# Six weight stores of a top-k attention and two-MLP kernel, moved from the preparation to the first product and behind a load of k

## The chip, the cores and the metric

The kernel runs on one core of a Trainium2 chip, as one launch. The metric is the device time of an execution in microseconds (us), and the median of several executions is compared. A core has five engines with instruction streams of their own: PE (matmul; its weight loads are shown as PEld), DVE (vector), ACT (scalar), POOL (GpSimd) and SP, which here issues every DMA. Each engine runs its stream strictly in the order in which it was written, and waits where an operand is not there yet.

## The reference

Attention in which each query keeps only its 32 largest scores, then two feed-forward layers without residuals.

```python
scores = scale * np.matmul(q, k.transpose(0, 1, 3, 2))     # 4 batches, 8 heads, 576 x 576, head size 64
kth = np.partition(scores, -top_k, axis=-1)[..., -top_k:-top_k + 1]
scores = np.where(scores >= kth, scores, -1000000000.0)
attn = softmax(scores)
x = np.matmul(attn, v)                                     # laid out as 2304 tokens x 512
h = x @ w_in;  x = (h - np.tanh(h)) @ w_out                # 512 -> 2048 -> 512
h = x @ w_in2; out = np.where(h > 0, h, np.exp(np.minimum(h, 0)) - 1) @ w_out2
```

The inputs of the attention are float32. The weights of the two layers are float64.

## The kernel before, in words

**Tiling.** The 2304 tokens are cut into 6 chunks of 384. For each chunk the attention is done pair of heads by pair of heads (4 pairs, two groups of three 128-row score tiles each), and then both layers run over 16 f-tiles of 128 columns each. The layers of a chunk run while the attention of the next chunk is under way. `m` is the layer (0 or 1), `ft` the f-tile, `ci` the chunk.

**Top-k.** For every score tile DVE takes four times the 8 largest values (`topk_steps`, L406) and three times removes them (L420); the threshold then masks the exponentials (`e`, L427 on DVE, L422/L423 on ACT). PE transposes `e` (L448), ACT copies it (`ph`, L449), PE multiplies with v (`av`, L470), and the normalized result is split into a high and a low part `xh`, `xl` (L148, L149).

**Weights.** PE works on words that are split into a high and a low part, which takes three products instead of one. `prepare(m, ft)` (L177 to L213) makes them once: SP loads the 1 MB of raw words `wr` (L180), ACT scales them (L186) and converts the low halves (L203), DVE joins both into `wf` (L189), ACT and POOL split that into `wp` (`split`, L147 to L149), and SP stores `wp`, 1 MB, to the DRAM scratch `w` (L213). Chunk 0 uses `wp` where it lies; chunks 1 to 5 load the words back as `wt` (`load_next`, L215, L222). `wp` and `wt` share one ring of `W2_BUFS` = 6 buffers (`weight_tile`, L172). So the seventh tile can only be written when the first is free: its product in `second` (L613) is done and every DMA that reads it has landed.

**Which tiles when.** Nine tiles (`EARLY`, numbers 12 to 20 of 32) are prepared in the first ticks and only stored. The first six of layer 0 (`AHEAD` = 6, `ft` 0 to 5) are prepared in the last ticks before the layers of chunk 0 begin, and stay in the ring. The rest follow while the layers of chunk 0 run: each step `c` of `step_parts` (L651) calls `first` of the next f-tile (L566; products `h`, L577, then `t`, L580), `gate` (L586), `second` (L602) and `load_next`.

**Loads of k.** `load_k` (L303) loads raw k as `kraw`; from chunk 1 on it comes in two halves (L316), in a ring of two buffers that is freed by the split into `kk`. `kraw1_1_1_0_0_1` is chunk 1, pair 1, batch 1, from query 0, head 1 of the pair; a number behind it in an order is the tile's running number. `sd`, `qraw`, `vraw` are the stores of parked scores and the loads of q and v.

**What sets the order.** The program writes the work in ticks (L731 to L773), and a scheduler then orders each engine's stream by its own estimate of when operands are ready. `tc.issue_after(x)`, used through `behind(kind)` (L153), keeps what is written under it behind `x` on its queue. A changed DMA thus also changes the order that the scheduler writes on the other engines. Once written, the order is fixed.

Of the kernel before, what the change touches and what calls it, by code (L numbers as in the profile page):

```python
# [19 lines left out]
B, H, S, D = 4, 8, 576, 64  # L20
# [7 lines left out]
NF = DFF // P  # L28
# [19 lines left out]

EARLY = range(12, 21)
PREP_AT = 8
PREP_RATE = 2.5
AHEAD = 6
# [52 lines left out]
def tile_topk_attention_two_mlps(  # L107
# [9 lines left out]
    nc = tc.nc  # L117
# [10 lines left out]
    def mlp_tile(shape, dt, **kw):  # L128
        if "open" in pools:
            opening.close()  # L130
            del pools["open"]
            pools["mlp"] = pool("mlp", 1)
        return pools["mlp"].tile(shape, dt, **kw)
# [10 lines left out]
    def f(ap):  # L144
        return ap.bitcast(F32)

    def split(hi, lo, src):  # L147
        nc.scalar.activation(hi, src, copy)  # L148
        return nc.gpsimd.tensor_sub(lo, src, f(hi))  # L149

    newest = {}

    def behind(kind):  # L153

        return tc.issue_after(newest[kind].ins) if kind in newest else nullcontext()

    def bank(tag, name, bufs):
        if tag == "h":
            if "park" in pairs:
                turns.close()  # L160
                del pairs["park"]
                pairs["h"] = pool("ph", 1, PSUM)
            return pairs["h"].tile([P, 512], F32, tag=tag, name=name, bufs=bufs)
        return ps.tile([P, 512], F32, tag=tag, name=name, bufs=bufs)


    scratch = {
        (m, ft): dr.tile([P, 2, 2, 512], F32R, tag=f"w{m}_{ft}", name=f"w{m}_{ft}") for m in range(2) for ft in range(NF)
    }
    weights, loads = {}, [(ci, m, ft) for ci in range(len(SIZES)) for m in range(2) for ft in range(NF)]  # L170

    def weight_tile(name):  # L172
        return sb.tile([P, 2, 2, 512], F32R, tag="w", name=name, bufs=W2_BUFS)
# [3 lines left out]
    def prepare(m, ft):  # L177

        raw = sb.tile([P, 1024], I64, tag="wr", name=f"wr{m}_{ft}", bufs=RAW_BUFS)
        nc.sync.dma_start(raw, (w1, w2)[m][ft])  # L180
        words = raw.bitcast(F32).rearrange("p (n w) -> p n w", w=2)
        low, scaled = words.bitcast(U32)[:, :, 0], words[:, :, 1]
        w = sb.tile([P, 1024], F32, tag="wf", name=f"wf{m}_{ft}", bufs=WF_BUFS)

        def scale(out, src):
            nc.scalar.activation(out, src, AF.Prelu, scale=2.0**-112, alpha=-(2.0**32))  # L186

        def join(out, high, low):
            nc.vector.scalar_tensor_tensor(  # L189
                out.bitcast(U32), high.bitcast(U32), 3, low, op0=ALU.logical_shift_left, op1=ALU.bitwise_or  # L190
            )

        halves = [slice(0, 512), slice(512, 1024)]
        small = {}
        early = "wide" in stage
        if early:
            for a, cs in enumerate(halves):
                small[a] = bank(f"acc{stage['at'] % 3}", f"sc{m}_{ft}_{a}", 1)
                stage["at"] += 1
                scale(small[a], scaled[:, cs])  # L200
        else:
            scale(scaled, scaled)
        nc.scalar.activation(low.bitcast(I32), low, copy, scale=2.0**-29 * (1 - 2.0**-20), bias=-0.5 + 7.5 * 2.0**-20)  # L203
        if early:
            for a, cs in enumerate(halves):
                join(w[:, cs], small[a], low[:, cs])
        else:
            join(w, scaled, low)
        wt = weight_tile(f"wp{m}_{ft}")
        if m * NF + ft not in EARLY:  # L210
            weights[0, m, ft] = wt
        split(wt[:, :, 0], wt[:, :, 1], w.rearrange("p (h c) -> p h c", h=2))
        nc.sync.dma_start(f(scratch[m, ft]), f(wt))  # L213

    def load_next():  # L215
        if loads:
            ci, m, ft = loads.pop(0)
            if ci == 0 and m * NF + ft not in EARLY:
                prepare(m, ft)
                return  # L220
            wt = weights[ci, m, ft] = weight_tile(f"wt{ci}_{m}_{ft}")
            newest["weights"] = nc.sync.dma_start(f(wt), f(scratch[m, ft]))  # L222
# [10 lines left out]
    for ci, size in enumerate(SIZES):  # L233
        for p in range(NPAIR):
            row = []
            c0 = 0
            for b, q0, n in CHUNKS[ci]:
                for heads in ([[0], [1]] if n >= 256 else [[0, 1]]):
                    u = Unit()
# [10 lines left out]
            cuts, k = [], 0  # L250
# [28 lines left out]
    def parked(u):  # L279

        return u.g.at in PARK
# [3 lines left out]
    def wide(u):  # L285

        return u.whole or parked(u)
# [15 lines left out]
    def load_k(u):  # L303
        if wide(u):
            if u.heads[0] == 0:
                tag, bufs = ("kp", 1) if parked(u) else ("kraw", KR_BUFS)
                k = pair_k[u.ci, u.p] = (pools["open"] if parked(u) else sb).tile([P, S], F32, tag=tag, name=f"kw{u.id}", bufs=bufs)
                for h in range(2):
                    nc.sync.dma_start(k[h * D : h * D + D], kT[u.b, 2 * u.p + h])
            u.kraw = pair_k[u.ci, u.p]  # L310
            return
        u.kraw = {}
        for h in u.heads:
            u.kraw[h] = sb.tile([P, S], F32, tag="kraw", name=f"kraw{u.id}_{h}", bufs=KR_BUFS)
            for half in range(2):
                nc.sync.dma_start(u.kraw[h][half * D : half * D + D], kT[u.b, 2 * u.p + h])  # L316

    def split_qk(u):

# [246 lines left out]
    def first(ci, m, ft):  # L566
        n = SIZES[ci]
        xh, xl = x_tiles[ci] if m == 0 else z_tiles[ci]
        h = bank("h", f"h{ci}_{m}_{ft}", 2)[:, :n]
        wv = weights[ci, m, ft][:, 0].rearrange("p a (k c) -> p a k c", c=P)  # L570
        jobs = [(wi, xs, kt) for wi, xs in ((0, xh), (1, xh), (0, xl)) for kt in range(4)]
        if m == 0 and ft == 0:
            jobs.sort(key=lambda x: x[2])
        late = (n // P - 1) * P
        for cs in (slice(0, late), slice(late, n)) if m == 1 and ft < PARTED and late else (slice(0, n),):
            for a, (wi, xs, kt) in enumerate(jobs):
                nc.tensor.matmul(h[:, cs], wv[:, wi, kt], xs[:, kt, cs], start=(a == 0), stop=(a == len(jobs) - 1))  # L577
        t = mlp_tile([P, NMAX], F32, tag="t", name=f"t{ci}_{m}_{ft}", bufs=T_BUFS)[:, :n]
        if m == 0:
            nc.scalar.activation(t, h, AF.Tanh)  # L580
        else:
            nc.scalar.activation(t, h, AF.Relu, scale=-1.0)  # L582
            nc.scalar.activation(t, t, AF.Exp, scale=-1.0)  # L583
        parts[ci, m, ft] = h, t
# [106 lines left out]
    for g in groups:  # L691
        t0 = 4 * g.at
        for u in g.units:
            lead = 6 if u.whole else 8
            if parked(u):
                at = PARK_AT + PARK_STEP * parks[0]
                parks[0] += 1
                on(before, int(at) - 3, lambda u=u: (load_q(u), load_k(u)))
                for t in range(u.k):
                    on(ends, int(at + t * PARK_STEP / 3), lambda u=u, t=t: later(park, u, t))  # L700
            else:
                on(before, max(-6, t0 - lead) if u.whole else t0 - lead, lambda u=u: (load_q(u), load_k(u)))
                on(before, t0 - 5, lambda u=u: split_qk(u))
            on(before, t0 + (1 if hurried(u) else 3), lambda u=u: load_v(u))
        for blk in range(NB):
            if not hurried(g.units[-1]):
                on(late, t0 + 4 + (1 if g.units[0].ci == 1 else 0) + (0 if quick(g.units[-1]) else blk // 3), lambda g=g, blk=blk: transposed(g, blk))
        for j, (u, t) in enumerate(g.tiles):
            on(mid, t0 - 4 + j, lambda u=u, t=t: scores(u, t))
        for u in g.units:  # L710
            if hurried(u):
                continue
            if u.last:
                on(ends, t0 + (5 if quick(u) else 7), lambda u=u: norm(u.ci, u.p, u))
                on(ends, t0 + (5 if quick(u) else 7), lambda u=u: attend(u))
                if spread(u):
                    on(ends, t0 + 8, lambda u=u: load_rs(u))
                    on(ends, t0 + 10, lambda u=u: finish_pair(u))
                else:
                    on(ends, t0 + (5 if quick(u) else 7), lambda u=u: finish_pair(u))  # L720
# [8 lines left out]

    early = list(EARLY)  # L730
    for tick in range(FIRST_TICK, n_ticks):  # L731
        for do in before.get(tick, ()):
            do()
        while early and PREP_AT + PREP_RATE * (len(EARLY) - len(early)) <= tick:
            i = early.pop(0)
            prepare(i // NF, i % NF)
        if starts[0] - AHEAD <= tick < starts[0]:
            load_next()
        if tick == starts[0]:
            first(*steps[0])  # L740
            gate(*steps[0])
# [71 lines left out]
```

## Time and profile before

| | |
|---|---|
| median of 3 runs | 1216.76 us (1215.71 to 1218.65) |
| profiled execution, its own time | 1219.57 us |
| its span, first to last instruction | 1217.8 us |
| PE busy | 1146.4 us (94%) |
| DVE busy | 944.5 us (78%) |
| ACT busy | 765.6 us (63%) |
| POOL busy | 497.9 us (41%) |
| bytes moved by DMA | 301.69 MB, mean 248 GB/s |

The profile shows one execution. Busy is the time in which an engine ran instructions; an idle engine waits for what the brackets in a timeline row name. Shares of the whole span mix stages with different limits, so stretches are read apart: the opening to about 160 us (attention of chunk 0 alone, weights prepared), the stretch to about 205 us in which the layers of chunk 0 start, and what follows. "Issue to landing" of a DMA is from its issue by SP until all of its bytes are there. "Granted clock" is TensorE's clock as the throttle granted it, as a share of full speed.

### The profile page before, as it was taken

To read this page: it belongs to the slowest core of one execution; us is meant where nothing else is said; L and a number is where in the kernel's file an instruction comes from. 1 tells how busy PE (TensorE), PEld (TensorE's weight loads), DVE (VectorE), ACT (ScalarE), POOL (GpSimd) and SP (SyncE) were. 2 spreads that over 40 slices of the span, in tenths; PEclk is the share of its full clock that TensorE was granted. 3 is DMA by queue.
4 is the path that set the end of the run, shared out by engine and by line. 5 is a ranking of instruction groups with operands and counts; after the bars stand their busy time and mean duration, and the time that the engine had idled before them with its cause. 6 is when DMAs were issued, how large, how long until landed. Compare 5 with 4: busy or idle time off the path is not lost.

```text
span 1217.8 us, 18856 instructions
## 1 busy us (share of the span) xinstructions
PE 1146.4 (94%) x6349; PEld 977.0 (80%) x6349; DVE 944.5 (78%) x1898; ACT 765.6 (63%) x1594; POOL 497.9 (41%) x557
## 2 busy tenths in 40 slices
PE   6577689999999999999999999999999999999998
PEld 3344368888888979898978988988998888898887
DVE  7999999998999999679987789898889995100111
ACT  5999987888984555565664566575655564432333
POOL 2445446657753313443423444444334422333222
PEclk9688889999999999999999999999999999999999
DMA  7999937985979986669986779978688645686572
GB/s 246 398 333 330 311 111 276 350 266 217 356 285 327 276 294 184 238 166 299 241 182 234 242 204 260 251 219 266 225 241 243 204 127 207 210 283 248 198 269 95
DMA packets 81616, 301.69 MB, mean 248 GB/s; under 512 B 18800, under 2 KB 36080, under 8 KB 51696
## 3 DMA queue, kind: packets, MB, share of 16 engines
q1 hardware_dynamic: 81520, 300.49, 76.5%
q8 instruction: 50, 0.82, 0.3%
q14 instruction: 46, 0.38, 0.1%
HBM read 255.07 MB, written 45.39 MB: 247 GB/s over the span
## 4 chain that ended last, share of the span: by engine, by line
PE 75%; ACT 6%; DVE 5%; DMA 3%; issue 1%; POOL 1%; another core or an unknown queue 0%; ACTq 0%; DVEq 0%; POOLq 0%
PE h L577 30%; PE acc L613 30%; PE av L470 6%; PE pt L448 5%; DMA wt<-w 3%; PE ps L383 2%; PE ps L384 2%; DVE vm L406 2%; DVE w L420 2%; DVE wf L189 1%; ACT ph L449 1%; ACT s L385 1%; ACT e L410 1%; ACT y L627 1%; ACT wr L186 0%
## 5 line engine op out<-in xcount | busy, mean ns | idle before, releaser
L149 POOL TENSOR_TENSOR gl<-g,gh 128x384 fp32r<-128x384 f32 x192 | 205.3, 1071 | 385.0 <-ACT gh L148 360.2
L406 DVE MAX8 vm<-w 128x8 f32<-128x576 f32 x432 | 315.0, 748 | 3.1
L613 PE MATMUL acc<-wt,gh 128*128 128x512 f32 x1014 | 270.9, 398 | 0.3 <-ACT gh L148 0.3
L613 PEld LDWEIGHTS acc<-wt,gh 128*128 128x128 f32 x1014 | 186.2, 188 | 34.9 <-issue 3.3
L420 DVE MATCH_REPLACE8 w<-vm,w 128x576 f32<-128x576 f32 x288 | 212.7, 740 | 0.0
L148 ACT ACTIVATE gh<-g 128x384 fp32r<-128x384 f32 x192 | 100.7, 525 | 81.2 <-DVE g L591 34.6
L613 PE MATMUL acc<-wt,gl 128*128 128x512 f32 x507 | 148.9, 398 | 1.0 <-POOL gl L149 1.0
L577 PE MATMUL h<-zh,wt 128*128 128x384 f32 (+2 forms) x776 | 146.4, 324 | 2.4 <-ACT zh L632 2.0
L591 DVE SCALAR_TENSOR_TENSOR g<-t,h 128x384 f32<-128x384 f32 x96 | 52.2, 544 | 124.2 <-ACT t L583 123.8
L406 DVE MAX8 vm<-s 128x8 f32<-128x576 f32 x144 | 107.2, 750 | 47.1 <-ACT s L385 44.4
L577 PE MATMUL h<-xh,wt 128*128 128x384 f32 x672 | 140.9, 339 | 1.2 <-DMA wt<-w 1.2
L385 ACT ACTIVATE s<-ps 128x288 f32<-128x288 f32 (+1 forms) x272 | 107.5, 418 | 48.3 <-PE ps L384 40.7
L449 ACT ACTIVATE ph<-pt 116x384 f32<-116x384 f32 (+1 forms) x240 | 111.5, 499 | 40.0 <-PE pt L448 37.4
L448 PE MATMUL pt<-ident,e 128*116 128x128 f32 (+1 forms) x720 | 115.2, 288 | 22.7 <-ACT e L423 9.9
L577 PEld LDWEIGHTS h<-zh,wt 128*128 128x128 f32 x776 | 125.8, 189 | 8.8 <-ACT zh L632 3.2
L448 PEld LDWEIGHTS pt<-ident,e 128*116 128x116 f32 (+1 forms) x720 | 90.0, 142 | 43.2 <-ACT e L423 12.6
L577 PEld LDWEIGHTS h<-xh,wt 128*128 128x128 f32 x672 | 117.4, 188 | 7.5 <-ACT t L580 1.0
L582 ACT ACTIVATE t<-h 128x384 f32<-128x384 f32 x96 | 46.8, 489 | 119.7 <-PE h L577 119.7
L613 PEld LDWEIGHTS acc<-wt,gl 128*128 128x128 f32 x507 | 93.3, 188 | 19.9 <-POOL gl L149 1.2
L420 DVE MATCH_REPLACE8 w<-vm,s 128x576 f32<-128x576 f32 x144 | 106.7, 741 | 0.0
L596 DVE TENSOR_TENSOR g<-h,t 128x384 f32<-128x384 f32 x76 | 41.4, 545 | 70.6 <-ACT t L580 69.9
L580 ACT ACTIVATE t<-h 128x384 f32<-128x384 f32 x96 | 47.2, 492 | 75.1 <-PE h L577 74.6
(82 smaller groups left out, 1938.7 us busy)
## 6 DMA issues: line engine op xcount, KB each, us to landing
wt<-w SPq DMA_DIRECT2D x169, 1024.0 KB, 6.5
wr<-in_w_dram SPq DMA_DIRECT2D x32, 1024.0 KB, 7.2
w<-wp SPq DMA_DIRECT2D x32, 1024.0 KB, 8.5
kraw<-in_kT_dram SPq DMA_DIRECT2D x96, 144.0 KB, 6.2
vraw<-in_vL_dram SPq DMA_DIRECT2D x64, 160.0 KB, 4.5
sd<-sp SPq DMA_DIRECT2D x24, 288.0 KB, 7.3
s<-sd SPq DMA_DIRECT2D x24, 288.0 KB, 9.0
qraw<-in_qT_dram SPq DMA_DIRECT2D x64, 96.0 KB, 5.7
```

The source lines that it names most:

```text
L148: nc.scalar.activation(hi, src, copy)
L149: return nc.gpsimd.tensor_sub(lo, src, f(hi))
L385: nc.scalar.activation(s[lo:hi, cs], pt[lo:hi, :HS], copy)
L406: nc.vector.max(g.vm[:, j, min(r, 1)], u.s[t] if r == 0 else g.w[j])
L420: nc.vector.match_replace(g.w[j], v, u.s[t] if r == 0 else g.w[j], FILL)
L448: nc.tensor.transpose(pt[:kn, j * P : j * P + P], v.e[t][:, k0 : k0 + kn], ident)
L449: nc.scalar.activation(g.ph[:kn, blk, :nq], pt[:kn, :nq], copy)
L470: nc.tensor.matmul(banks[c0][h * D : h * D + D, : v.n], v.vraw[h][:kn, blk], v.g.ph[:kn, blk, cs], start=(blk == order[0]), stop=(blk == o ...
L577: nc.tensor.matmul(h[:, cs], wv[:, wi, kt], xs[:, kt, cs], start=(a == 0), stop=(a == len(jobs) - 1))
L580: nc.scalar.activation(t, h, AF.Tanh)
L591: nc.vector.scalar_tensor_tensor(g, t, -1.0, h, op0=ALU.add, op1=ALU.max)
L613: nc.tensor.matmul(acc[ci, m][t], gx[:, t * P : t * P + P], wt[:, wi], start=(ft == 0 and k == 0), stop=(ft == NF - 1 and k == 2),)
```

## The change

For the tiles with a number under `AHEAD` (layer 0, `ft` 0 to 5) `prepare` no longer issues the store but keeps the tile in `kept`. `first(ci, m, ft)` issues it when the tile's first product is written, under `behind("k")`, so behind the half of a `kraw` tile that was written last by then. The other 26 stores stay in `prepare`. No instruction is added or taken away.

```diff
--- before.py
+++ after.py
@@ -48,7 +48,7 @@
 
 
 
-EARLY = range(12, 21)
+EARLY = range(12,21)
 PREP_AT = 8
 PREP_RATE = 2.5
 AHEAD = 6
@@ -210,7 +210,12 @@
         if m * NF + ft not in EARLY:
             weights[0, m, ft] = wt
         split(wt[:, :, 0], wt[:, :, 1], w.rearrange("p (h c) -> p h c", h=2))
-        nc.sync.dma_start(f(scratch[m, ft]), f(wt))
+        if m * NF + ft < AHEAD:
+            kept[m, ft] = wt
+        else:
+            nc.sync.dma_start(f(scratch[m, ft]), f(wt))
+
+    kept = {}
 
     def load_next():
         if loads:
@@ -313,7 +318,7 @@
         for h in u.heads:
             u.kraw[h] = sb.tile([P, S], F32, tag="kraw", name=f"kraw{u.id}_{h}", bufs=KR_BUFS)
             for half in range(2):
-                nc.sync.dma_start(u.kraw[h][half * D : half * D + D], kT[u.b, 2 * u.p + h])
+                newest["k"] = nc.sync.dma_start(u.kraw[h][half * D : half * D + D], kT[u.b, 2 * u.p + h])
 
     def split_qk(u):
 
@@ -568,6 +573,9 @@
         xh, xl = x_tiles[ci] if m == 0 else z_tiles[ci]
         h = bank("h", f"h{ci}_{m}_{ft}", 2)[:, :n]
         wv = weights[ci, m, ft][:, 0].rearrange("p a (k c) -> p a k c", c=P)
+        if (m, ft) in kept:
+            with behind("k"):
+                nc.sync.dma_start(f(scratch[m, ft]), f(kept.pop((m, ft))))
         jobs = [(wi, xs, kt) for wi, xs in ((0, xh), (1, xh), (0, xl)) for kt in range(4)]
         if m == 0 and ft == 0:
             jobs.sort(key=lambda x: x[2])
```

The first place is SP's queue. Before, the stores of tiles 0 to 5 (`w0_0` to `w0_5`) stand one by one among the loads of the opening; the last three of them:

```order
L213 DMA w0_3_80<-wp0_3_1469 128x2048
L295 DMA qw2_3_1_192_1_1048<-in_qT_dram 64x384
L301 DMA qraw1_0_0_384_0_1003<-in_qT_dram 64x2x192 x2
L180 DMA wr0_6_1650<-in_w1_dram 128x1024
L213 DMA w0_4_81<-wp0_4_1506 128x2048
L356 DMA sd2_3_1_192_0_2_1177<-sp2_3_1_192_0_2_1172 128x576
L316 DMA kraw1_0_1_0_0_0_1182<-in_kT_dram 64x576 x2
L180 DMA wr0_7_1733<-in_w1_dram 128x1024
L301 DMA qraw1_0_1_0_0_1179<-in_qT_dram 64x2x192 x2
L213 DMA w0_5_82<-wp0_5_1544 128x2048
L356 DMA sd2_3_1_192_1_0_1245<-sp2_3_1_192_1_0_1240 128x576
L180 DMA wr0_8_1798<-in_w1_dram 128x1024
```

Now the six stand far behind `wr0_9`, and the queue runs so around them:

```order
L321 DMA kraw1_1_1_0_0_1_1561<-in_kT_dram 64x576 x2
L578 DMA w0_0_77<-wp0_0_1305 128x2048
L578 DMA w0_1_78<-wp0_1_1349 128x2048
L578 DMA w0_2_79<-wp0_2_1377 128x2048
L578 DMA w0_3_80<-wp0_3_1466 128x2048
L578 DMA w0_4_81<-wp0_4_1502 128x2048
L321 DMA kraw1_2_0_384_0_0_1876<-in_kT_dram 64x576 x2
L306 DMA qraw1_2_1_0_0_2188<-in_qT_dram 64x2x192 x2
L321 DMA kraw1_2_0_384_0_1_1879<-in_kT_dram 64x576 x2
L578 DMA w0_5_82<-wp0_5_1539 128x2048
```

Five stores follow one another behind the second half of `kraw1_1_1_0_0_1`, ahead of the next k; the sixth stands two k tiles further on. The loads `wr0_3` to `wr0_9` moved up: `wr0_8` and `wr0_9` now stand ahead of `kraw1_0_1_0_0_1`.

The second place is DVE at the end of chunk 0's last group (names with `0_3`), into which the first group of chunk 1 (`1_0`) is woven. Before:

```order
L406 MAX vm0_3_0_3_0_0_1_1202<-w30_3_0_3_0_0_1_2_1207 128x8
L406 MAX vm1_0_1_0_0_384_0_1441<-s1_0_0_384_0_0_1213 128x8
L420 MATCH_REPLACE w30_3_0_3_0_0_1_2_1207<-vm0_3_0_3_0_0_1_1202,w30_3_0_3_0_0_1_2_1207 128x576
L420 MATCH_REPLACE w31_0_1_0_0_384_0_0_1444<-vm1_0_1_0_0_384_0_1441,s1_0_0_384_0_0_1213 128x576
L406 MAX vm0_3_0_3_0_0_1_1202<-w30_3_0_3_0_0_1_2_1207 128x8
L406 MAX vm1_0_1_0_0_384_0_1441<-w31_0_1_0_0_384_0_0_1444 128x8
L427 SCALAR_TENSOR_TENSOR e0_3_0_0_1_2_1251,sum0_3_0_3_0_0_1_1204<-s0_3_0_0_1_2_1102,vm0_3_0_3_0_0_1_1202,e0_3_0_0_1_2_1251 128x576
L420 MATCH_REPLACE w31_0_1_0_0_384_0_0_1444<-vm1_0_1_0_0_384_0_1441,w31_0_1_0_0_384_0_0_1444 128x576
L501 RECIPROCAL r0_3_1413<-r0_3_1413 128x6
```

And now:

```order
L411 MAX vm1_0_1_0_0_384_0_1438<-w31_0_1_0_0_384_0_0_1441 128x8
L411 MAX vm1_0_1_0_0_384_0_1438<-s1_0_0_384_0_1_1259 128x8
L411 MAX vm0_3_0_3_0_0_1_1202<-w30_3_0_3_0_0_1_2_1207 128x8
L425 MATCH_REPLACE w31_0_1_0_0_384_0_0_1441<-vm1_0_1_0_0_384_0_1438,w31_0_1_0_0_384_0_0_1441 128x576
L411 MAX vm1_0_1_0_0_384_0_1438<-s1_0_0_384_0_2_1312 128x8
L425 MATCH_REPLACE w31_0_1_0_0_384_0_1_1442<-vm1_0_1_0_0_384_0_1438,s1_0_0_384_0_1_1259 128x576
L432 SCALAR_TENSOR_TENSOR e0_3_0_0_1_2_1251,sum0_3_0_3_0_0_1_1204<-s0_3_0_0_1_2_1102,vm0_3_0_3_0_0_1_1202,e0_3_0_0_1_2_1251 128x576
L411 MAX vm1_0_1_0_0_384_0_1438<-w31_0_1_0_0_384_0_0_1441 128x8
L425 MATCH_REPLACE w31_0_1_0_0_384_0_2_1443<-vm1_0_1_0_0_384_0_1438,s1_0_0_384_0_2_1312 128x576
L411 MAX vm1_0_1_0_0_384_0_1438<-w31_0_1_0_0_384_0_1_1442 128x8
L506 RECIPROCAL r0_3_1410<-r0_3_1410 128x6
```

The last mask `e0_3_0_0_1_2` went from place 206 to 210 of DVE's stream, the reciprocal `r0_3` from 208 to 214, and `xl0` (the end of chunk 0's attention) from 227 to 230, since more rows of `1_0` stand ahead of them.

The third place is ACT where the ninth and tenth tile are split (`wp0_8`, `wp0_9`) and the layers of chunk 0 are at f-tile 4 and 5. Before:

```order
L148 ACTIVATE kk1_2_0_384_0_0_2092<-kraw1_2_0_384_0_0_1877 128x576
L449 ACTIVATE ph1_0_1_0_0_384_0_1708<-pt1_0_1_0_0_384_0_3_1779 116x384
L148 ACTIVATE wp0_8_1804<-wf0_8_1800 128x2x512
L580 ACTIVATE t0_0_4_1836<-h0_0_4_1823 128x384
L148 ACTIVATE wp0_9_1870<-wf0_9_1866 128x2x512
L449 ACTIVATE ph1_0_1_0_0_384_0_1708<-pt1_0_1_0_0_384_0_4_1784 112x384
L186 ACTIVATE wr0_10_1935<-wr0_10_1935 128x1024
L203 ACTIVATE wr0_10_1935<-wr0_10_1935 128x1024
L580 ACTIVATE t0_0_5_1902<-h0_0_5_1889 128x384
```

And now:

```order
L148 ACTIVATE wp0_8_1802<-wf0_8_1798 128x2x512
L588 ACTIVATE t0_0_4_1835<-h0_0_4_1821 128x384
L454 ACTIVATE ph1_0_1_0_0_384_0_1705<-pt1_0_1_0_0_384_0_3_1777 116x384
L454 ACTIVATE ph1_0_1_0_0_384_0_1705<-pt1_0_1_0_0_384_0_4_1782 112x384
L148 ACTIVATE kk1_2_0_384_0_0_2092<-kraw1_2_0_384_0_0_1876 128x576
L427 ACTIVATE e1_0_1_0_0_0_1656<-s1_0_1_0_0_0_1449,nk1_0_1_0_1_0_0_1819 128x576
L427 ACTIVATE e1_0_1_0_0_1_1657<-s1_0_1_0_0_1_1477,nk1_0_1_0_1_0_0_1819 128x576
L415 ACTIVATE e1_1_0_384_0_2_1947<-s1_1_0_384_0_2_1760,mb1_1_1_1_0_384_0_1883 128x576
L148 ACTIVATE wp0_9_1869<-wf0_9_1865 128x2x512
L428 ACTIVATE e1_0_1_0_0_0_1656,sum1_0_1_0_1_0_0_1592<-e1_0_1_0_0_0_1656,b21_0_1_0_1_0_0_1820 128x576
L588 ACTIVATE t0_0_5_1902<-h0_0_5_1888 128x384
```

Between `wp0_9` and `t0_0_5` one `e` stands instead of one `ph` and both conversions of `wr0_10`, which went 17 places further down; `kk1_2_0_384_0_0` moved behind `wp0_8`, and three `e` moved ahead of `wp0_9`.

On every engine the order differs from the opening to the third chunk's layers, and is the same from there to the end.

## Rows read from the trace of the kernel before

**Rows 1.** The page: DMA share in 40 slices of 30.4 us, stores (KB each, us to landing).

```profile
DMA  7999937985979986669986779978688645686572
...
w<-wp SPq DMA_DIRECT2D x32, 1024.0 KB, 8.5
```

**Rows 2.** Windows: stretch, length, busy of PE, PEld, DVE, ACT, POOL, clock, DMA, GB/s.

```profile
80.00:150.00 70.00, 48.00 (x187) 29.09 (x186) 67.04 (x128) 67.66 (x132) 33.09 (x41) 0.84 0.94 335
150.00:190.00 40.00, 35.64 (x185) 29.43 (x186) 38.04 (x78) 32.36 (x67) 20.57 (x22) 0.89 0.39 123
210.00:640.00 430.00, 424.33 (x2516) 367.24 (x2517) 393.81 (x798) 289.86 (x601) 194.84 (x223) 1.00 0.83 263
640.00:1217.80 577.80, 569.01 (x3210) 503.92 (x3206) 355.30 (x724) 296.39 (x646) 207.43 (x220) 1.00 0.71 223
...
80.00:160.00 80.00, 56.17 (x229) 36.25 (x228) 77.04 (x150) 76.14 (x146) 36.82 (x44) 0.83 0.90 318
160.00:205.00 45.00, 39.70 (x201) 33.13 (x202) 43.04 (x78) 34.49 (x73) 27.20 (x27) 0.92 0.49 162
```

**Rows 3.** Timeline, ACT then DVE, 117 to 125: start, us, instruction, [idle before, releaser].

```profile
117.01 0.65 ACT L354 ACTIVATE sp<-pp 128x576 f32<-128x576 f32 x1 [1.28 <-issue]
...
119.81 1.23 DVE L189 SCALAR_TENSOR_TENSOR wf<-wr 128x1024 uint32<-128x1024 uint32 x1 [1.51 <-issue]
...
124.44 0.76 DVE L406 MAX8 vm<-s 128x8 f32<-128x576 f32 x1 [0.55 <-ACT s L385]
```

**Rows 4.** Groups by form on DVE, 60 to 260: busy us, mean ns, idle.

```profile
L406 DVE MAX8 vm<-w 128x8 f32<-128x576 f32 x94 | 68.3, 747 | 0.5
L420 DVE MATCH_REPLACE8 w<-vm,w 128x576 f32<-128x576 f32 x62 | 45.8, 740 | 0.0
```

**Rows 5.** Timeline of ACT, 183 to 202.

```profile
183.91 1.06 ACT L148 ACTIVATE wp<-wf 128x1024 fp32r<-128x1024 f32 x1 [0.21 <-PE acc L613]
...
186.99 1.06 ACT L148 ACTIVATE wp<-wf 128x1024 fp32r<-128x1024 f32 x1 [0.31 <-PE acc L613]
...
191.06 0.69 ACT L148 ACTIVATE kk<-kraw 128x576 fp32r<-128x576 f32 x1
...
197.79 1.06 ACT L148 ACTIVATE wp<-wf 128x1024 fp32r<-128x1024 f32 x1 [4.33 <-DVE wf L189]
...
199.12 1.15 ACT L186 ACTIVATE wr<-wr 128x1024 f32<-128x1024 f32 x1
200.16 1.16 ACT L203 ACTIVATE wr<-wr 128x1024 int32<-128x1024 uint32 x1
201.22 0.48 ACT L580 ACTIVATE t<-h 128x384 f32<-128x384 f32 x1
```

**Rows 6.** Timeline of PE, 199 to 238.

```profile
199.28 0.48 PE L383 MATMUL ps<-kk,qs 128*128 128x288 f32 x1 [2.24 <-ACT ph L449]
...
228.12 3.48 PE L470 MATMUL av<-ph,vraw 116*64 116x192 f32 x40
...
237.58 0.34 PE L577 MATMUL h<-xh,wt 128*128 128x384 f32 x1
```

**Rows 7.** Timeline of the SP queue: first and last of six stores, one k tile.

```profile
94.27 0.32 SPq L213 DMA_DIRECT2D w<-wp  x1
...
136.14 0.33 SPq L213 DMA_DIRECT2D w<-wp  x1
...
174.75 1.52 SPq L316 DMA_DIRECT2D kraw<-in_kT_dram  x2
```

**Rows 8.** By line or tile, issue to landing: stores 80-260, `wt` whole span, `kraw` 150-200.

```profile
DMA to landing us min/median/max: 7.9/8.8/9.7
...
DMA to landing us min/median/max: 4.7/6.5/16.0
...
DMA to landing us min/median/max: 2.6/2.7/2.8
```

**Rows 9.** Waits of the SP queue, 90 to 200: total, times, longest.

```profile
SPq L316 <- POOL kk L149: 16.5, 5, 6.1
```

## The prediction

> **What bounds the kernel now.** I read the windows by stretch first [rows 2]. From 210 us on PE is busy for 424.33 of 430 us, and from 640 on for 569.01 of 577.8: the rest of the program is PE's work, one piece behind another, and a microsecond that PE is ahead or behind at about 205 arrives at the end. Before that PE has no work to fill its time. From 80 to 160 DVE is busy for 77.04 of 80 us and ACT for 76.14; PE waits for them. From 160 to 205, where the layers of chunk 0 begin, PE lacks 45 - 39.70 = 5.30 us and DVE 1.96.
>
> DMA is the third full resource of the opening. Its 16 engines are busy for 0.94 of 80 to 150 at 335 GB/s, and then for 0.39 of 150 to 190 at 123 GB/s; the page's row shows the same hole in its sixth slice, a 3 between nines [rows 1, 2]. The six stores are issued between 94.27 and 136.14 [rows 7], in the full part, and the change puts them into the hole. So the question is not whether DMA is relieved, which it is, but who waits for it while DVE and ACT are full as well. Then I read the timelines for that.
>
> **The change, part by part.** A store is 1024 KB, 1.05 MB; at 335 GB/s it takes 3.1 us of all engines, the six 18.8 us. Times are on the profiled execution, 1219.57 us (span 1217.8), which is 2.8 above the median; differences are carried over to the median, 1216.76.
>
> 1. *The stores leave the opening.* In 80 to 160 DVE idles 80 - 77.04 = 2.96 us in all. One gap looks like DMA's: ACT's 1.28 us at 117.01, where it copies parked scores into one of two buffers, with no engine named, while the store of the older one is under way; DVE's 1.51 at 119.81 and 0.55 at 124.44 stand behind it [rows 3]. I take **-1.3**, ACT's gap, since DVE's follow from it. Ends: 0 and -2.96. The rest of the 18.8 us is covered by DVE's and ACT's own work.
>
> 2. *The end of chunk 0 moves back on DVE.* `xl0`, with which the layers' input is complete, stands three rows of top-k further down, `r0_3` six. A row is 0.747 or 0.740 us [rows 4]: 3 x 0.74 = 2.2, 6 x 0.74 = 4.5. They are work of chunk 1, which DVE saves later, but PE begins the layers later by it. I take **+2.2**, as `xl0` is what the products need; ends 0 (DVE's waits there take it up) and +4.5. ACT has a like cost in the same place: the conversions of `wr0_8` and `wr0_9`, 2 x (1.15 + 1.16) = 4.6 us by the rows of `wr0_10` [rows 5], now run ahead of the end of chunk 0, but other ACT work went behind it, so it lies within these ends.
>
> 3. *The preparation between f-tiles 4 and 5.* Before, ACT stands still for 4.33 us in front of `wp0_9` (197.79), then runs both conversions of `wr0_10`, 1.15 and 1.16, and only then `t0_0_5` (201.22) [rows 5]. PE waits 2.24 us at 199.28 for the copy `ph` behind `wp0_9` [rows 6]. In the new order that `ph`, a `kk` and three `e` stand ahead of `wp0_9`, and the conversions 17 places down. I take **-2.2**, PE's wait; ends 0 (`wf0_9` itself comes later) and -5.3 (all that PE lacks from 160 to 205).
>
> 4. *The ring.* `wp0_6` (183.91) and `wp0_7` (186.99) start 0.21 and 0.31 us after PE freed a buffer [rows 5]; now they need `w0_0` and `w0_1` to have landed as well, and all of ACT is queued behind them. The stores follow `kraw1_1_1_0_0_1`, issued from 174.75 to 176.3 [rows 7]. A 1 MB transfer lands after 4.7 us at the fastest (`wt`), a store in the full stretch after up to 9.7 [rows 8]: 181.0 or 186.0, a stall of 0 or 2.1. In the hole k's halves land after 2.6 to 2.8 us, so the fast end is the nearer one, and I take **0**; ends 0 and +2.1. `w0_1`, 3.1 us behind, asks nothing more: 189.1 against 186.99 + 2.1.
> The Trainium skill, page "DMA: Bandwidth & Descriptors", section "Rules for kernel authors", says to issue a DMA early, compute, and wait for its semaphore late; the change does the reverse with six stores whose landing frees a buffer. By that rule the upper end would hold here, and the sum would be 1217.6; no row of before shows such a late store.
>
> 5. *What is queued behind the stores on SP.* `kraw1_2_0_384_0_0` now follows five of them: 176.3 + 5 x 3.1 + 2.7 = 194.5, where its split stood at 191.06 on ACT [rows 5, 8]. In the new order two `ph`, `wp0_8` and `t0_0_4` come first, and an empty queue may run faster than 335. I take **0**; ends 0 and +3.4. `w0_5`, `w0_6` and `wr0_10` come some microseconds later; their users stand further down. `wt0_0_12` now stands behind loads of v that wait for `av1_0_0`. Before, `av` of that pair ends at 228.12 + 3.48 = 231.6 and `wt0_0_12` is needed at 237.58 [rows 6], 6.0 us for a landing of 6.5 in the median [rows 8]; but on PE `av1_0_0` moved 8 places up and the user 10 down, so **0**, ends 0 and +0.5.
>
> 6. *The order from 210 to the third chunk* is written anew on all engines. PE idles 5.67 us there [rows 2]; I take **0**, ends half of that either way, 2.8.
>
> Sum: -1.3 + 2.2 - 2.2 = -1.3, so 1218.3 for the profiled execution and **1215.5** for the median. A measurement of this kernel can tell about 0.2%, 2.4 us, from no change.
>
> **The rivals.**
> *The gaps go.* If DMA's load is behind more of DVE's gaps than the one I can name, and the new order closes PE's as well: -2.96 - 5.30 + 2.2 = -6.1, 1210.7. For it speaks that DMA is as full as DVE; against it that in 80 to 160 only 4% of DVE's time is idle at all.
> *The late stores hold the ring.* Place: ACT at `wp0_6`. It decides if `w0_0` lands later than 183.9, 7.6 us after its issue. Price: 2.1 there, and the 2.2 of `xl0` with nothing won in part 3, as ACT stands: +4.3, 1221.1; with the k of part 5 in place of the ring (3.4) and DVE's other rows, up to +7.9. For it: stores in the full stretch took 7.9 to 9.7 [rows 8], and the time to spare is small. Against: the hole.
> *The stores miss the hole.* SP waits for POOL to free k's buffers, 16.5 us in five waits, the longest 6.1 [rows 9]. If such a wait grows by 6.1 ahead of the stores, `w0_0` lands at 187.1, +3.2 at `wp0_6`: -1.3 + 3.2 = +1.9, 1218.7.
>
> **How the numbers follow.** My forecast 0.38, the gaps go 0.36, the ring 0.22, the hole missed 0.04 (half of it within 0.2%). So faster by over 0.2%: 0.36; within 0.2%: 0.40; slower: 0.24. The forecast's own range is 1213 to 1219. Signs are mixed, so the range takes in both rivals: down to 1210.7 and 1.2 of part 6, up to 1221.1 and 1.4 of it: 1209.5 to 1222.5.
>
> **What would show it.** GB/s of 80 to 150 falls by about 6.3 MB / 70 us = 90, and 150 to 190 rises by 6.3 / 40 = 157. SP issues `w0_0` at 176 to 178. Part 1: no gap of ACT near 117. Part 2: `xl0` and the layers' first products come up to 2 us later. Part 3: no PE gap near 199. Part 4: PE, not DMA, releases `wp0_6`. I am wrong if `wp0_6` waits for a store, if DVE's idle time in the opening stays and the time still falls by over 2.4 us, or if PE's idle time after 210 changes by more than 2.8.

## The result and the profile after

The changed kernel takes 1225.18 us in the median of four executions (1223.93 to 1228.99), the kernel before beside it 1216.61: a ratio of 1.0073 with a 95% interval of 1.0047 to 1.0100, so **slower by 0.7%, 8.6 us**. Run again later with more executions it gave 1.0068 (1.0054 to 1.0082); that run is called e13 below. The forecast was 1215.5 with a range up to 1222.5: wrong in sign and outside the range.

The profiled execution after took 1228.99 us (span 1227.2), 3.8 above its median. Windows of the changed kernel, as in [rows 2] (stretch, length, busy of PE, PEld, DVE, ACT, POOL, clock, DMA, GB/s):

```profile
80.00:150.00 70.00, 47.71 (x168) 30.16 (x166) 64.48 (x120) 66.64 (x124) 34.02 (x39) 0.78 0.79 272
150.00:190.00 40.00, 32.66 (x165) 23.53 (x165) 38.66 (x79) 29.45 (x71) 13.59 (x19) 0.84 0.26 80
80.00:160.00 80.00, 57.23 (x211) 35.37 (x210) 73.98 (x139) 74.77 (x142) 35.86 (x42) 0.77 0.73 249
160.00:205.00 45.00, 38.14 (x204) 31.53 (x203) 44.16 (x89) 31.70 (x71) 25.07 (x23) 0.92 0.50 177
210.00:640.00 430.00, 422.45 (x2463) 363.49 (x2464) 391.03 (x781) 284.88 (x594) 198.20 (x221) 1.00 0.86 270
```

DMA was relieved from 80 to 150 (335 GB/s to 272), but the hole behind it did not fill: 123 fell to 80. DVE, the full engine of the opening, has lost 3 us of work in 80 to 160 (77.04 to 73.98). From 210 to 640 PE is busy 1.9 us less than before (422.45 against 424.33 in [rows 2]); in e13 it is as busy as before (424.93). The SP queue of the changed kernel, against [rows 7], tells why the hole stayed empty:

```profile
185.25 1.32 SPq L321 DMA_DIRECT2D kraw<-in_kT_dram  x2
186.62 4.71 SPq L578 DMA_DIRECT2D w<-wp  x5
```

The k in front of the stores is issued at 185.25 instead of 174.75, the stores 10 us later than forecast. So the end of chunk 0's attention is late already. DVE of the changed kernel at the fifth join of the opening, at `xl0` and at the layers' first `g`:

```profile
33.55 0.69 DVE L189 SCALAR_TENSOR_TENSOR wf<-sc,wr 128x512 uint32<-128x512 uint32 x1 [4.61 <-ACT wr L203]
...
181.63 0.55 DVE L561 TENSOR_TENSOR xl<-xun,xh 128x384 fp32r<-128x384 f32 x1
...
185.08 0.54 DVE L604 TENSOR_TENSOR g<-h,t 128x384 f32<-128x384 f32 x1
```

The last two in the kernel before:

```profile
171.91 0.55 DVE L556 TENSOR_TENSOR xl<-xun,xh 128x384 fp32r<-128x384 f32 x1
...
175.94 0.53 DVE L596 TENSOR_TENSOR g<-h,t 128x384 f32<-128x384 f32 x1
```

`xl0` is 9.7 us later, the first `g` 9.1. This execution was 3.1 us late already at the fifth join (33.55 against 30.44), where raw words landed late, ahead of the first instruction whose order differs. e13 has that join at 31.02, `xl0` at 181.03 and `g` at 184.47, 8.5 later, and ends at 1223.6. So a lag is there **before the layers of chunk 0 begin**. PE does not simply carry it to the end: in e13 the eighth `g` is 1.5 us behind the kernel before (215.98 against 214.52), the end of chunk 0's first layer 6.3 (271.64 against 265.32) and the end of the span 5.8, since behind `xl0` too the order is another. The ring did not hold anything. ACT of the changed kernel at `wp0_6` and `wp0_7`:

```profile
193.67 1.06 ACT L148 ACTIVATE wp<-wf 128x1024 fp32r<-128x1024 f32 x1
...
196.09 1.06 ACT L148 ACTIVATE wp<-wf 128x1024 fp32r<-128x1024 f32 x1 [0.27 <-PE acc L621]
```

### The profile page after: what moved, and what is told of

Same layout as the page of the kernel before. It is cut to its first block, busy times and chain, and to the rows that moved or that the text cites. A ratio compares the mean times of both kernels' runs of the same rounds, so it can differ in the third digit from the quotient of the medians.

```text
span 1227.2 us, 18861 instructions
## 1 busy us (share of the span) xinstructions
PE 1150.9 (94%) x6349; PEld 976.0 (80%) x6349; DVE 949.3 (77%) x1898; ACT 762.9 (62%) x1594; POOL 504.3 (41%) x557
## 4 chain that ended last, share of the span: by engine, by line
PE 60%; ACT 3%; DVE 1%; DMA 1%; issue 1%; POOL 0%; ACTq 0%; POOLq 0%; DVEq 0%
PE acc L621 25%; PE h L585 25%; PE av L475 4%; PE pt L453 3%; PE ps L388 2%; PE ps L389 1%; DVE vm L411 1%; DMA s<-sd 1%; ACT y L635 1%; ACT e L415 1%; ACT ph L454 1%; ACT zh L640 0%; DVE w L425 0%; ACT s L390 0%; ACT t L591 0%
## 5 line engine op out<-in xcount | busy, mean ns | idle before, releaser
L411 DVE MAX8 vm<-w 128x8 f32<-128x576 f32 x432 | 319.3, 749 | 3.6
```

Source lines behind the costliest of these rows:

```text
L411: nc.vector.max(g.vm[:, j, min(r, 1)], u.s[t] if r == 0 else g.w[j])
```

## The experiments

Two things changed at once: when six transfers run, and the order that the scheduler wrote on every engine. Theory O says that the order costs the time, theory S that the late stores do. All ratios are to the kernel before, run beside it on the same chip; the medians come from several chips and are not to be compared across groups of runs.

| run | opening's order | order behind it | six stores | median us | ratio (95%) |
|---|---|---|---|---|---|
| e1 | new | its own | none | 1235.18 | 1.0140 (1.0114 to 1.0166) |
| e2 | held 7 to 9 | its own | late | 1227.69 | 1.0077 (1.0056 to 1.0099) |
| e3 | held 6 to 9 | its own | late | 1231.08 | 1.0109 (1.0087 to 1.0131) |
| e4 | held 6 to 9 | its own | at once | 1230.90 | 1.0109 (1.0084 to 1.0134) |
| e5 | old | old | late | 1222.65 | 1.0033 (1.0021 to 1.0045) |
| e6 | new | new | at once | 1233.86 | 1.0126 (1.0103 to 1.0148) |
| e7 | old | old | in the hole | 1220.90 | 1.0022 (1.0009 to 1.0035) |
| e8 | old | old | none | 1217.20 | 0.9990 (0.9974 to 1.0007) |
| e9 | new | old | late | 1229.88 | 1.0105 (1.0089 to 1.0120) |
| e10 | old | new | late | 1222.16 | 1.0046 (1.0032 to 1.0060) |
| e11 | of e4, to f-tile 8 | old | at once | 1220.40 | 1.0035 (1.0022 to 1.0048) |
| e12 | of e4, to layer 0's end | old | at once | 1216.43 | 0.9993 (0.9984 to 1.0003) |
| e13 | new | new | late | 1225.02 | 1.0068 (1.0054 to 1.0082) |
| e14 | of e2 | new | late | 1225.00 | 1.0075 (1.0060 to 1.0089) |
| e15 | new | new | none | 1226.82 | 1.0057 (1.0038 to 1.0076) |
| e16 | of e2 | new | none | 1224.25 | 1.0050 (1.0037 to 1.0064) |

**e1, e2, e3, e4: the scheduler left free.** e1 leaves out the six stores, and chunks 1 to 5 load the words of tiles 6 to 11 in place of those of tiles 0 to 5, as many bytes (e8, e15 and e16 do the same; their times count, not what they compute):

```diff
-            with behind("k"):
-                nc.sync.dma_start(f(scratch[m, ft]), f(kept.pop((m, ft))))
+            kept.pop((m, ft))
...
-            newest["weights"] = nc.sync.dma_start(f(wt), f(scratch[m, ft]))
+            newest["weights"] = nc.sync.dma_start(f(wt), f(scratch[m, ft + 6 if m == 0 and ft < 6 else ft]))
```

> Left out: the six stores of tiles 0 to 5 altogether (chunks 1 to 5 load the words of tiles 6 to 11 in their place). The order of every engine's stream is that of the changed kernel up to the first f-tiles of chunk 0's layers. Theory O (the new order of the opening costs the time: the conversions of wr0_3 to wr0_9 stand ahead of chunk 0's last group): the first g of chunk 0 is computed at about 182 to 185 us, as in the changed kernel without its disturbed opening, and the time is 1221 to 1226. Theory S (the stores cost it, by where they land: the ring, k and the raw words behind them): nothing is left to wait for, 1214 to 1218.

It took 1235.18 us, by the ratios 0.67% or 8 us more than with the stores (1.0140 against 1.0073), which theory S cannot explain; nor is it what theory O said, since the scheduler wrote the rest anew as well. The others hold conversions back on ACT, e2 behind the first exponentials of chunk 0's last group, e3 and e4 behind its last `xh`:

```diff
+        held = (lambda: behind("e")) if m == 0 and ft in (7, 8, 9) else nullcontext
...
-            scale(scaled, scaled)
-        nc.scalar.activation(low.bitcast(I32), low, copy, scale=2.0**-29 * (1 - 2.0**-20), bias=-0.5 + 7.5 * 2.0**-20)
+            with held():
+                scale(scaled, scaled)
+        with held():
+            nc.scalar.activation(low.bitcast(I32), low, copy, scale=2.0**-29 * (1 - 2.0**-20), bias=-0.5 + 7.5 * 2.0**-20)
```

> The stores stay late; both conversions of wr0_7, wr0_8 and wr0_9 on ACT are held behind the first exponentials of chunk 0's last group. Theory O: the first g of chunk 0 comes back to 176 to 179 us, the time to 1215 to 1219. Theory S: the stores are as late as in the changed kernel, so 1222 to 1226.

> The stores stay late; both conversions of wr0_6 to wr0_9 are held until chunk 0's attention is complete (behind the last xh). Theory O: the first g of chunk 0 at 174 to 177 us, but then four tiles of conversions, 4 x 2.3 us, stand on ACT beside the first f-tiles, and the seventh tile's words come late: 1214 to 1220. Theory S: 1222 to 1226.

> The kernel before, with its stores at once, and the same hold as in the run above (conversions of wr0_6 to wr0_9 behind the last xh). Theory O: what the hold gives is independent of the stores, so this stands within 2 us of the held kernel with late stores, 1213 to 1219. Theory S: this one has its stores early, and is 6 to 9 us faster than the held kernel with late stores.

The opening answered as theory O said: `xl0` at 170.7, 169.4 and 165.2. The times did not: all three were 9 to 13 us slower than the kernel before. e4 was early at `xl0` and lost it from 260 to 350 us, where PE is busy for 79.68 us against 87.17 in the kernel before. Its longest wait there is for a copy of scores:

```profile
280.12 0.61 PE L386 MATMUL ps<-kk,qs 128*128 128x288 f32 x1 [5.06 <-ACT s L388]
```

So a kernel that is left to the scheduler does not test the stores or the opening by themselves: each edit brings a new order behind the opening as well, with stalls of its own.

**e5 to e8: the order pinned.** From here each instruction is tied behind the one that is to stand ahead of it on its engine. The tie sets the order of issue only:

```diff
+    streams = {}
+    for i in nc.cur_bb.bb.instructions:
+        if i.name.startswith("I-") and type(i).__name__.startswith("Inst"):
+            streams.setdefault(str(i.engine).split(".")[-1], []).append(i)
+    keep = mybir.DependencyInfo(mybir.DependencyClass.NoSync, mybir.DependencyReason.DATA)
+    for engine, places in ORDER.items():
+        line = [streams[engine][p] for p in places]
+        for x, y in zip(line, line[1:]):
+            tc.add_manual_dep(y, x.name, keep, reason="order")
```

`ORDER` holds each engine's stream as place numbers, read from a built kernel. With it the stores can move alone, or the order alone; only the table and the place of the stores differ from here on. The tables hold SP's stream too, so "new" takes in the changed kernel's order of the loads; the order is tested as a whole, not engine by engine.

> The streams of PE, DVE, ACT and POOL stand word for word in the order of the kernel before, each instruction tied behind the one ahead of it; on SP's queue the six stores alone are moved, to where the changed kernel has them (five behind the second half of kraw1_1_1_0_0_1, the sixth behind kraw1_2_0_384_0_1). Theory O (the order that the scheduler wrote anew costs the time): 1214 to 1219, within 2 us of the kernel before. Theory S (the late stores cost it): 1221 to 1226, with ACT waiting for a store at wp0_6.

> The mirror image: PE, DVE, ACT and POOL in the order of the changed kernel, and on SP's queue the six stores back at the places where their words are ready, between 97 and 131 us. Theory O: as slow as the changed kernel, 1222 to 1228; the first g of chunk 0 at 181 to 185 us. Theory S: 1214 to 1219.

> The order of the kernel before on the four engines, all six stores behind the second half of kraw1_1_0_384_0_1 on SP, at about 150 to 160 us, early in the stretch in which DMA is busy for 0.39. Theory O: 1213 to 1218; wp0_6 does not wait, and k's next loads behind six stores are at most 3 us later. Theory S: the stores are 20 us earlier than in the changed kernel, so the ring is free, but k waits: 1217 to 1222.

> Left out: the six stores (chunks 1 to 5 load the words of tiles 6 to 11 in their place); the order of the kernel before on the four engines. It shows what the six stores cost where they stood. Theory O: what DMA gives back is ACT's gap at 117 at most, 1213 to 1218. Theory S: as soon as the stores are gone from everywhere, the time falls below the kernel before by more than 3 us, under 1214.

e5 moves the six transfers and nothing else. It costs 0.33%, 4 us: more than theory O said, at the lower end of theory S, and not at the ring where theory S put it. ACT and PE of e5:

```profile
183.68 1.06 ACT L152 ACTIVATE wp<-wf 128x1024 fp32r<-128x1024 f32 x1 [0.21 <-PE acc L625]
...
193.52 0.69 ACT L152 ACTIVATE kk<-kraw 128x576 fp32r<-128x576 f32 x1 [2.57 <-DMA kraw<-in_kT_dram]
...
201.97 1.13 ACT L190 ACTIVATE wr<-wr 128x1024 f32<-128x1024 f32 x1 [4.74 <-DMA wr<-in_w_dram]
...
196.12 0.30 PE L392 MATMUL ps<-kk,qs 128*128 128x288 f32 x1
...
206.13 0.61 PE L392 MATMUL ps<-kk,qs 128*128 128x288 f32 x1 [5.66 <-ACT s L394]
```

`wp0_6` starts as before, released by PE. Then ACT waits 2.57 us for the k behind the stores and 4.74 for the raw words of tile 10, which SP issued at 192.00, behind the sixth store (189.13); DMA is busy for 0.97 of 190 to 195, against 0.50 in the kernel before. PE waits 5.66 for the copy behind those words. Not all of the 4.74 is new: the kernel before stood 4.33 at `wp0_9`, just ahead of this conversion [rows 5], so the conversion itself comes 2.85 later (201.97 against 199.12). e7 issues the stores into the hole itself, at 159.8 to 165.6, and pays with a k again:

```profile
ACT kk L152 <- DMA kraw<-in_kT_dram: 5.6, 1, 5.6
```

e8 shows that where the stores stood they cost nothing that can be told from no change, with DMA at 260 GB/s from 80 to 150 instead of 335. e6 is the mirror of e5: the new order with the stores back at once is 1.26% slower, 15 us. Its waits from 80 to 160 on ACT and on DVE (total, times, longest):

```profile
ACT wr L190 <- DMA wr<-in_w_dram: 6.9, 6, 2.5
...
DVE vm L410 <- ACT s L389: 9.8, 6, 4.7
```

The same in e13, the changed kernel:

```profile
ACT wr L186 <- DMA wr<-in_w_dram: 6.0, 3, 3.4
...
DVE vm L411 <- ACT s L390: 6.4, 5, 3.0
```

And in the kernel before, where ACT waits for no raw words in this stretch:

```profile
ACT sp L354 <- issue: 1.3, 1, 1.3
...
DVE vm L406 <- ACT s L385: 1.2, 2, 0.6
```

This is how `xl0` comes late. In the new order the conversions of `wr0_3` to `wr0_9` stand further ahead in ACT's stream. ACT runs in order, and where the raw words have not landed it stands, with the copies of scores behind it that DVE and PE need. The longest such wait of e13, at the conversion of `wr0_9`, with DVE and PE behind it:

```profile
144.41 1.12 ACT L186 ACTIVATE wr<-wr 128x1024 f32<-128x1024 f32 x1 [3.40 <-DMA wr<-in_w_dram]
...
148.47 0.76 DVE L411 MAX8 vm<-s 128x8 f32<-128x576 f32 x1 [3.01 <-ACT s L390]
...
147.89 1.53 PE L453 MATMUL pt<-ident,e 128*116 128x128 f32 x6 [4.83 <-ACT ph L454]
```

The load of `wr0_9` on SP in e13, then load and conversion in the kernel before:

```profile
135.72 0.33 SPq L180 DMA_DIRECT2D wr<-in_w_dram  x1
```

```profile
151.29 0.54 SPq L180 DMA_DIRECT2D wr<-in_w_dram  x1
...
157.83 1.12 ACT L186 ACTIVATE wr<-wr 128x1024 f32<-128x1024 f32 x1
```

The load moved up by 15.6 us. ACT began to wait at 141.0, 16.8 ahead of where the conversion ran before, and without a wait.

**e9, e10: which part of the order.** Same tie; the seam is `xl0`.

> Stores late as in the changed kernel. On every engine, what the kernel before has up to xl0 (the end of chunk 0's attention) stands in the changed kernel's order, all that follows in the order of the kernel before. Theory P (the opening's new order costs 5 to 6.5 us, and the late stores 4 in the old order behind it): the first g of chunk 0 at 181 to 185 us, the time 8 to 11 us over the kernel before, 1226 to 1230. Theory R (the rest's new order is the cost, the opening's lag is taken up again): 3 to 5 us over, 1221 to 1224.

> The mirror image: stores late, the opening up to xl0 in the order of the kernel before, all that follows in the changed kernel's order. Theory P: the first g at 175 to 177 us; the new rest has wr0_10's conversions 17 rows further down and so waits less for them than the old one did with late stores; 0 to 3 us over the kernel before, 1217 to 1222. Theory R: 6 to 9 us over, 1224 to 1228.

With the old order behind it the new opening costs 0.72% (1.0105 against e5's 1.0033), 8.8 us, as theory P said. With the new order behind it, it costs 0.22%, 2.7 us (1.0068 against 1.0046), with intervals that touch. The prices do not add: the new rest takes up part of a late start. That the rest's new order is the whole cost falls: e10 is 4.8 us over the kernel before, past the 0 to 3 of theory P and short of the 6 to 9 of theory R, and against e5 the new rest costs 0.13%, within the intervals.

**e11, e12: a faster version?**

> Stores at once. Up to the first product of f-tile 8 the order of the run with stores at once and held conversions (e4), which was 3 us of PE's work ahead of the kernel before at 240 us and fell back only between 270 and 330; behind it the order of the kernel before. If e4's loss lay in its own later order (theory P): 1 to 4 us under the kernel before, 1214 to 1217. If a lead at 240 us is lost again whatever the order, because something else (raw words, DMA) bounds 270 to 330: 1218 to 1222.

> The same with the seam at the end of layer 0 of chunk 0 (first copy y), where e4 was 6 us ahead of the kernel before. Theory P: 2 to 6 us under the kernel before, 1212 to 1216. If 270 to 330 is bounded by something else: 1218 to 1224.

Neither beats the kernel before. e12, which ends layer 0 of chunk 0 3 us earlier (262.2 against 265.3), takes the same time; e11 is slower. A lead at one point is not yet a gain.

**e13 to e16: is it those conversions, and what do the late stores cost in the new order?**

> The changed kernel itself, unedited, as the ground for the next run: 0.5 to 1.0% over the kernel before, 1223 to 1229; the first g of chunk 0 5 to 8 us later than before, counted from the fifth join wf of the opening.

> The changed kernel's order everywhere, late stores too, but up to xl0 the order of the run with held conversions (e2): those of wr0_7, wr0_8 and wr0_9 stand behind the first exponentials of chunk 0's last group. If these conversions, written ahead of that group, are what the opening's new order costs: the first g at 175 to 179 us, the time 3 to 7 us under the changed kernel, 0 to 4 us over the kernel before. If another part of the opening's order costs it (the parked scores, the rows of chunk 1): within 2 us of the changed kernel.

> Left out: the six stores (chunks 1 to 5 load the words of tiles 6 to 11 in their place); the changed kernel's order on PE, DVE, ACT and POOL, from beginning to end. It shows what the late stores cost in that order. If they cost there what they cost in the old order, 3 to 5 us under the changed kernel, 1220 to 1223; if the new order leaves room for them (wr0_10's conversions stand 17 rows further down), within 2 us of it, 1223 to 1227.

> The same with the held opening (e14 without its stores). If the late stores swallowed the lead of 5.9 us: the eighth g of chunk 0 at 209 to 213 us and 3 to 6 us under the run with the changed order and no stores. If the held conversions and PE's clock swallow it: the eighth g within 2 us of that run's, and the time too.

e15 settles the stores: the new order without any store is as slow as with them late (1.0057 against 1.0068 and 1.0073, within the intervals). Against e8, the old order without any store, it is 1.0057 / 0.9990 = 1.0067, 8 us. **The order by itself is enough for the cost.** The prices do not add here either: with the late stores in both, the new order costs 0.35% (1.0068 against e5's 1.0033).

e15 also bounds what the raw words explain. Its ACT waits for them from 80 to 160 less than half as long as e13's, and its `xl0` is hardly earlier:

```profile
ACT wr L190 <- DMA wr<-in_w_dram: 2.4, 1, 2.4
...
180.38 0.55 DVE L565 TENSOR_TENSOR xl<-xun,xh 128x384 fp32r<-128x384 f32 x1
```

Some 2.3 us of its lateness were there at the fifth join (33.27 against 31.02 in e13); the time is the same.

e14 differs from the changed kernel only up to the first products of chunk 0's layers, mostly in places of DVE's and ACT's streams, in fewer of PE's, POOL's and SP's. Against e13 its `xl0` comes 6.0 us earlier, but its first `g` only 2.7:

```profile
175.07 0.54 DVE L565 TENSOR_TENSOR xl<-xun,xh 128x384 fp32r<-128x384 f32 x1
...
181.75 0.54 DVE L608 TENSOR_TENSOR g<-h,t 128x384 f32<-128x384 f32 x1
```

By the eighth `g` nothing is left (215.9 against 216.0), and the time is the same, though e14's profiled execution is 4.6 us above its median. In e16 against e15, without the stores, `xl0` comes 7.4 us earlier and the eighth `g` 2.2, and the times (1.0050, 1.0057) lie within each other's intervals. That the late stores swallowed the lead falls with that, and that these three tiles' conversions are the whole cost as well. Where the lead went is shown in part. From `xl0` to the first `g` DVE takes 6.7 us in e14 and 3.4 in e13, in e14 without a gap: rows of chunk 1's top-k that stood ahead of `xl0` now stand behind it, and still ahead of the `g`. Windows of e13, then of e14, around the first products:

```profile
180.00:185.00 5.00, 3.76 (x22) 3.40 (x22) 4.90 (x12) 4.90 (x15) 1.66 (x2) 1.00 0.02 3
185.00:190.00 5.00, 5.00 (x32) 4.99 (x31) 5.00 (x12) 4.92 (x13) 4.33 (x5) 1.00 0.73 275
```

```profile
180.00:185.00 5.00, 3.37 (x12) 3.07 (x13) 4.97 (x11) 3.00 (x8) 4.13 (x5) 0.55 0.69 264
185.00:190.00 5.00, 5.00 (x24) 4.87 (x24) 5.00 (x11) 2.96 (x6) 1.85 (x3) 0.77 1.00 419
```

In e14 TensorE's granted clock is 0.55 and 0.77 there, after PE was busy for 2.71 of the 5 us from 175 to 180, and PE gets through 36 instructions in the time of 54. In e16 the clock is 0.50 from 180 to 185. The rest of the lead is not traced, and which rows of the new order would have to move back for the time to come back stays open.

## Why the prediction was wrong

**The price of the order failed, first of all in part 2.** Parts 2, 3 and 6 price the new order, and came to +2.2 - 2.2 + 0 = 0; by e15 against e8, with no store in either, it is 8 us. The first term that is seen to fail is part 2. It said that `xl0` moves back by three rows of top-k, +2.2 with an upper end of 4.5; measured in e13 it is 9.1 (181.03 against 171.91). Windows of e13 from the start to the end of `xl0`, and of the kernel before:

```profile
0.00:181.60 181.60, 123.30 (x447) 75.99 (x448) 161.04 (x317) 149.77 (x289) 68.69 (x92) 0.81 0.71 251
```

```profile
0.00:172.50 172.50, 119.92 (x454) 76.42 (x454) 157.94 (x313) 150.56 (x291) 69.01 (x92) 0.83 0.85 300
```

DVE ran 3.1 us more work ahead of `xl0` (161.04 - 157.94, four instructions more): that is the term I counted, nearly right. It also stood 6.0 us longer (20.56 against 14.56), and that term was missing. In the profiled execution after the two are 5.0 and 4.7 (162.92 busy of 182.20), so the split between them is rough. The sentence that failed is the last of part 2: "other ACT work went behind it, so it lies within these ends". I weighed ACT's moved rows by their duration, and never asked whether the raw words would have landed where the rows now stood. The order, which I had, showed the conversions of `wr0_8` and `wr0_9` ahead of the exponentials of chunk 0's last group; from issue to landing of the raw words I read no row. That part 2 alone decides the time is not shown: in e14 `xl0` is 3.2 us late (175.07), within its ends, and the time is as long. The new opening costs 8.8 us with the old order behind it (e9 against e5) but 0.22%, 2.7 us, with the new one (e13 against e10, whose intervals still touch), so by which rows the rest of the 8 us comes stays open. The premise that a microsecond of PE at about 205 arrives at the end did not hold in e4, where the order behind was new too: it lost its lead from 260 to 350.

**Part 1** took -1.3 for the stores' leaving. e8 gives 0.9990 with 1 inside its interval: no gain that can be told; e8 still has ACT's gap of 1.3 at the parked copy, so the load of the six stores on DMA was not behind it. **Part 3** was right that PE's gap at 199 goes, but one of 2.36 us comes at 210.58 in e13, and from 160 to 205 PE is busy for 37.71 us there against 39.70, so nothing was won. **Part 4** was right: `wp0_6` and `wp0_7` never waited for a store, in e5 (0.21, PE) or in the changed kernel. The rule of the Trainium skill that was weighed there, from "DMA: Bandwidth & Descriptors", section "Rules for kernel authors", to issue a DMA early and wait for it late, spoke against the change. In the old order the late stores do cost 4 us (e5), but not by the stall at the ring that was drawn from the rule: what came late was the k and the raw words behind the stores. **Part 5** said 0 for these, with an upper end of 3.4 for the k and none for the raw words. In the old order e5 shows 2.57 and 4.74 on ACT and +4.0 in all; in the changed kernel's order, where these users stand further down, nothing that can be told (e13 against e15). **Part 6** took 0 within 2.8: e10 against e5 is 0.13%, within their intervals. A small misreading beside it: in the page's row the 3 stands between a 9 and a 7, not between nines.

**The rivals.** "The late stores hold the ring" had the nearest time, 1221.1, for a mechanism that did not happen. Its longer form, up to +7.9, comes near the 8.6 by luck: it needs the k behind the stores, and in the new order late stores cost nothing that can be told; and the range stopped short of it at 1222.5. "The stores miss the hole" did happen, by 10 us instead of 6.1, but as a consequence: ahead of the k in front of the stores SP stood 7.9 us for PE's `av` and up to 7.2 for POOL's split of k (e13), both part of the late attention. "The gaps go" fell: DVE's idle time in the opening grew. The missing rival was the order written anew as a cause of its own, with the point from which it decides: a row that moves ahead of the landing of its operand.

**What was to show it.** The fall of GB/s from 80 to 150 came (90 forecast; 63 in the profile after, 76 in e13), the rise from 150 to 190 did not, and the issue of `w0_0` at 186.6 instead of 176 to 178 was the first sign that the opening, not the stores, was at fault. `xl0`, "up to 2 us later" in the forecast, was 9. None of the three conditions under "I am wrong if" came about: none of them asked for a late opening.

## What to carry to other kernels

Where a moved DMA makes a scheduler write a new order, price the order as a change of its own: for each engine that runs in order, ask of every row that moved ahead whether its operand has landed by then, and who stands behind it. To learn what a transfer costs, pin the order of the other engines and move the transfer alone; without that, one edit changes hundreds of places at once. And a gain at a milestone in the middle (`xl0` 6.0 us earlier in e14) is no gain at the end until a run shows it there.

## What was not expected of the hardware

The same six stores of 1 MB cost nothing in one order and 8 us in another. At once in the old order they stand at 1 / 0.9990 against none, within the interval; at once in the new order at 1.0126 / 1.0057 = 1.0069 against none. The bytes and the queue are the same. What differs in the rows is how long ACT stands for raw words from 80 to 160: 6.9 us in e6 against 2.4 in e15, with `xl0` at 186.17 against 180.38; in the old order it stands for them 0 us with the stores at once. That this is all of the 8 us is not shown.

PE pays for a wait twice. In e5 a score product takes 0.30 us at 196.12, and 0.61 at 206.13, behind the wait of 5.66 us. The granted clock of the stretch from there, in e5's windows, is 0.50, which is the level of 1.2 GHz:

```profile
205.00:210.00 5.00, 3.75 (x10) 2.93 (x11) 5.00 (x12) 4.97 (x13) 1.25 (x2) 0.50 1.00 375
```

The Trainium skill, page "TensorE: Matmul & The Clock Gate", section "What's actually happening", names these two levels and ties the lower one to an idle array; the rows agree.
